# Three first attention tiles in another layout, with the first weight slice converted among their masks

## The chip, the cores and the metric

The kernel runs on one core of a Trainium2 chip. That core has five engines that run side by side and wait for each other through semaphores: PE (matrix products; PEld is its loading of weights), DVE (VectorE), ACT (ScalarE), POOL (GpSimd) and SP, which here only issues transfers (DMAs). Each engine takes its instructions in the order in which they were written. The metric is the device time of the whole kernel in microseconds (us).

## What is computed

The reference has three parts, one after the other:

```python
for t in range(S):                      # attention with decay, per batch and head
    cur = u * kt (x) vt
    y[:, :, t] = rt @ (state + cur)
    state = w * state + kt (x) vt
x = (silu(x @ w_gate) * (x @ w_val)) @ w_out          # 3072 x 384, d_ff 1536
...
e_idx = argmax(x @ gate)                              # 8 experts, one for each token
out[mask] = gate_w * eom * (relu(x[mask] @ w1[e]) @ w2[e])
```

Batch 4, 8 heads of 48, 768 positions: 3072 tokens, 24 tiles of 128. What matters here is the term with `u`, called the bonus: a token's own key and value count with the factor `u`, so a score matrix of a tile has, on its diagonal, the sum over the 48 features of r * u * k, and above it the decayed scores of the earlier tokens of the tile.

## The kernel before

Attention runs over tiles of 128 tokens. For a tile, the transposed keys and queries (features on the partitions) are scaled by powers of the decay `w` (table `WT`, built by `decay_tables` on DVE), PE makes the scores of 8 heads in two PSUM banks (`a_scores`), the diagonal of bonus sums is laid into `at` (`a_diag`: identity times the sum of a head, eight rows on ACT or one operation on POOL), DVE copies the scores over it where the mask allows (`a_mask`), and PE multiplies with v (`a_out_mm`, head pair 3 first, since its result is spread by ACT and a shift product over the three other pairs). ACT's cast and DVE's difference (`a_out_ev`) split the result into a high and a low half for the first FFN. Its twelve weight slices come as 64-bit words; DVE turns each into 32 bits (`conv_steps`: three steps of three integer operations), ACT and POOL split it (`conv_b`), PE turns its gate part (`gate_a`, `gate_b`).

Tiles 0 to 2 are handled before the first FFN block, in a layout of their own: the keys of odd and even heads lie in two separate halves with zeros in the other rows, so a score product uses all 128 rows, and each tile takes two scalings, of 1024 and of 512 columns (`a_scale`). The bonus sums are made from natural r and k, token by token: two POOL products (`a_bonus`) and a DVE sum. Later tiles have one scaling, and their score products use 64 rows each.

No planner sets the order: under `manual_schedule` each engine does its work in the order of the calls in the main function, and inside the blocks in the order of the lists `slots`. Transfers stand in SP's order, and a transfer there waits for its target to be free. Numbers behind names in the rows of the order are buffers: `bank_61` to `bank_68` are the PSUM banks 0 to 7. The names used below: `krT`, `kr3` scaled keys and queries; `rkv` natural r, k, v; `kp`, `Wk` the table that scales natural keys for the state, made by `key_table`; `raw` a weight slice as loaded, `cv` converted.

## Time and profile before

| | us |
|---|---|
| median of three runs | 863.32 (859.99 to 863.79) |
| profiled execution | 861.56 |
| its span | 859.8 |
| PE busy in the span | 821.9 (96%) |
| DVE / ACT / POOL busy | 459.8 / 271.2 / 267.9 |

The profile is of one execution. Times in it count from the start of its span; 1.76 us lie around the span. A busy share over the whole span is a mean over stages with different limits, so the rows below are read by stretches: the start with three attention tiles, the stretch in which DVE converts the weight slices, and the rest.

### The profile page before, as it was taken

Reading aid. Unit: us, or ns where it says so; the run is one execution under the profiler, and the core shown is the slowest. Engines: PE = TensorE matmul, PEld = TensorE weight load, DVE = VectorE, ACT = ScalarE, POOL = GpSimd, SP = SyncE. Lnnn points to the kernel's source line nnn. Section 1 sums busy time; section 2 is a strip of 40 time slices with the busy share of each in tenths; the row PEclk is TensorE's granted clock in tenths of the full one; section 3 lists DMA queues with packets and bytes.
Section 4 is the critical chain, followed back from the end, with each engine's and each line's share of the span. In section 5 each row is a group of like instructions: output and inputs, shape, how many; then the busy total and the mean of one; then the engine's idle time right before and its main releaser. Section 6 shows DMA issues by size and latency. Waiting matters only on the chain.

```text
span 859.8 us, 13873 instructions
## 1 busy us (share of the span) xinstructions
PE 821.9 (96%) x5427; PEld 792.9 (92%) x5427; DVE 459.8 (53%) x945; ACT 271.2 (32%) x590; POOL 267.9 (31%) x241
## 2 busy tenths in 40 slices
PE   2888889999999999999999999999999999999996
PEld 2677789999999999999999999999999999999996
DVE  7898753354465456456455434243565565465541
ACT  2434342221222212212212221223454454444432
POOL 6756546223425335245244112010110210121022
PEclk9879989999999999999999999999999999999999
DMA  8615413853322323333323210410394444444201
GB/s 249 247 59 209 146 67 100 249 141 123 105 94 78 129 78 107 109 102 130 116 102 130 60 47 29 161 51 1 118 368 142 167 142 127 158 133 163 85 26 36
DMA packets 29769, 104.90 MB, mean 122 GB/s; under 512 B 5175, under 2 KB 14193, under 8 KB 26624
## 3 DMA queue, kind: packets, MB, share of 16 engines
q1 hardware_dynamic: 26368, 94.37, 34.0%
q0 software_dynamic: 3328, 9.56, 2.9%
q8 instruction: 45, 0.74, 0.4%
q14 instruction: 28, 0.23, 0.1%
HBM read 85.84 MB, written 16.41 MB: 119 GB/s over the span
## 4 chain that ended last, share of the span: by engine, by line
PE 84%; DVE 8%; DMA 2%; issue 2%; ACT 1%; SPq 1%; POOL 0%; POOLq 0%; DVEq 0%; ACTq 0%
PE bank L494 31%; PE bank L513 17%; PE bank L708 12%; PE bank L725 12%; PE bank L363 3%; PE bank L390 2%; PE bank L376 2%; DVE bank L215 2%; DVE bank L214 2%; DMA spare<-in_rkv_dram 2%; DVE cv L216 2%; PE bank L673 1%; PE bank L739 1%; SPq L415 1%; DVE krT L316 1%
## 5 line engine op out<-in xcount | busy, mean ns | idle before, releaser
L494 PE MATMUL bank<-xT,W 128*128 128x384 f32 x1728 | 331.4, 342 | 1.5 <-DMA xT<-stage 1.3
L494 PEld LDWEIGHTS bank<-xT,W 128*128 128x128 f32 x1728 | 305.1, 189 | 5.8 <-DMA xT<-stage 2.2
L513 PE MATMUL bank<-W,h 128*128 128x400 f32 x864 | 176.0, 348 | 0.0
L513 PEld LDWEIGHTS bank<-W,h 128*128 128x128 f32 x864 | 155.9, 189 | 0.5 <-issue 0.2
L505 ACT CAST h<-s 128x384 fp32r<-128x384 f32 x96 | 49.2, 513 | 328.4 <-DVE s L503 328.4
L503 DVE TENSOR_TENSOR s<-s,bank 128x384 f32<-128x384 f32 x96 | 53.2, 554 | 161.4 <-PE bank L494 148.6
L725 PE MATMUL bank<-hd,wf 128*128 128x416 f32 (+1 forms) x576 | 113.9, 344 | 0.0
L725 PEld LDWEIGHTS bank<-hd,wf 128*128 128x128 f32 x576 | 104.3, 188 | 0.7 <-DVE hd L712 0.2
L747 POOL DMA_INDIRECT out_dram<-yo,ix x32 | 35.0, 1095 | 200.6 <-DVE yo L743 174.0
L343 POOL TENSOR_TENSOR at<-ident,a 128x1024 f32<-128x1024 f32 x19 | 36.1, 1897 | 149.2 <-PE bank L494 118.2
L712 DVE SCALAR_TENSOR_TENSOR hd<-bank,hd 128x416 fp32r<-128x416 f32 (+1 forms) x64 | 36.7, 573 | 77.1 <-ACT hd L711 77.1
L506 DVE TENSOR_TENSOR h<-s,h 128x384 fp32r<-128x384 f32 x84 | 51.8, 616 | 48.7 <-ACT h L505 48.7
L657 DVE TENSOR_TENSOR wf<-raw,wf 128x768 fp32r<-128x768 f32 x64 | 61.1, 955 | 7.0 <-ACT wf L656 1.2
L502 ACT ACTIVATE s<-bank 128x384 f32<-128x384 f32 x96 | 47.2, 492 | 47.4 <-PE bank L494 47.4
L575 POOL DMA_INDIRECT xs<-rows,slot x24 | 23.8, 991 | 112.8 <-DVE slot L573 51.5
L711 ACT ACTIVATE hd<-bank 128x416 fp32r<-128x416 f32 (+1 forms) x64 | 32.3, 505 | 82.3 <-PE bank L708 81.9
L708 PE MATMUL bank<-xd1h,wf 128*128 128x416 f32 x192 | 58.2, 361 | 0.0
L656 ACT CAST wf<-raw 128x768 fp32r<-128x768 f32 x64 | 52.8, 825 | 0.0
L368 DVE COPY_PREDICATED at<-mask,bank 128x512 f32<-128x512 int32 x42 | 28.5, 732 | 38.7 <-POOL at L343 35.3
L708 PE MATMUL bank<-xd0h,wf 128*128 128x416 f32 x144 | 43.8, 362 | 0.0
L708 PEld LDWEIGHTS bank<-xd1h,wf 128*128 128x128 f32 x192 | 36.0, 188 | 0.5
L324 POOL TENSOR_TENSOR rkv<-rkv,ub 128x384 f32<-128x384 f32 x21 | 21.8, 1037 | 46.3 <-DMA rkv<-in_rkv_dram 46.3
(175 smaller groups left out, 946.9 us busy)
## 6 DMA issues: line engine op xcount, KB each, us to landing
raw<-in_w_dram SPq DMA_DIRECT2D x36, 768.0 KB, 4.4
raw<-in_w_dram SPq DMA_DIRECT2D x22, 1152.0 KB, 7.1
rkv<-in_rkv_dram SPq DMA_DIRECT2D x21, 576.0 KB, 5.4
krT<-in_krT_dram SPq DMA_DIRECT2D x42, 192.0 KB, 3.4
xs<-zt SPq DMA_DIRECT2D x32, 197.0 KB, 6.0
xr<-xs SPq DMA_DIRECT2D x6, 591.0 KB, 5.7
spare<-in_w_dram SPq DMA_DIRECT2D x2, 1152.0 KB, 9.4
xT<-stage SPq DMA_DIRECT2D x42, 48.0 KB, 2.1
```

The lines of the kernel that those rows point to most:

```text
L343: pool.tensor_tensor(out=af, in0=bc(ident, 1, [P, NH, P]), in1=bc(a, 2, [P, NH, P]), op=ALU.mult)
L494: pe.matmul(ps[i], W[f][:, wl, o : o + P], x[:, xl, c, :], start=(c == 0 and n == 0), stop=(c == KC - 1 and n == 2),)
L502: act.activation(out=s, in_=g, func=AF.Silu)
L503: dve.tensor_tensor(out=s, in0=s, in1=v, op=ALU.mult)
L505: act.copy(out=h[:, 0], in_=s)
L506: (pool if blk == 0 else dve).tensor_tensor(out=h[:, 1], in0=s, in1=h[:, 0].bitcast(F32), op=ALU.subtract)
L513: pe.matmul(bank[t][:, 0 : DM + 16], h[:, hl, t * P : (t + 1) * P], W[f][:, wl, 2 * KC * P :], start=(f == 0 and n == 0), stop=(f == NF - ...
L656: act.copy(out=wf[:, 0], in_=raw[:, f])
L657: dve.tensor_tensor(out=wf[:, 1], in0=raw[:, f], in1=wf[:, 0].bitcast(F32), op=ALU.subtract)
L708: pe.matmul(ps, wf[:, wl, c * P : (c + 1) * P], xd[xl][:, c, 0:n], start=(i == 0), stop=(i == 3 * KC - 1))
L712: dve.scalar_tensor_tensor(h[:, 1, 0:n], ps, 0.0, h[:, 0, 0:n].bitcast(F32), ALU.max, ALU.subtract)
L725: pe.matmul(bank[c][:, 0:n], wf[:, wl, o : o + P], h[:, hl, 0:n], start=(f == 0 and i == 0), stop=(f == NEF - 1 and i == 2),)
```

## The change

Tiles 0 to 2 get the layout of the later tiles: odd and even heads in the two halves of the rows, one load for each half, one scaling of 1024 columns, score products of 64 rows. Natural r is not loaded for them. The bonus sums come from the scaled k and r: POOL multiplies the two (`pr3`), and PE sums over the features with four products a tile whose other operand is `uw`, u times w, into eight columns of bank 7 (`a_same`); a copy takes them out (`a_same_copy`). The natural v and k come as loads of their own behind the first weight slice. The three tiles go in step through scaling, scores, sums, diagonals, masks and outputs, and the three conversion steps of weight slice 0 stand among the masks and outputs. The table `kp` and `Wk`, and two of four memsets of the state, are made later; the memset of the third tile's buffer goes from POOL to DVE.

```diff
+    uT = cst.tile([P, 4], F32, name="uT")
+    uw = cst.tile([P, 4, 2], F32, name="uw")
...
-    kr3 = [spare[NF - 1 - i][:, 0 : 12 * P].rearrange("s (a p t) -> s a p t", a=3, p=4) for i in range(3)]
+    kr3 = [spare[NF - 1 - i][:, 0 : 8 * P].rearrange("s (a p t) -> s a p t", a=2, p=4) for i in range(3)]
+    pr3 = [spare[NF - 1 - i][:, 8 * P : 12 * P].rearrange("s (p t) -> s p t", p=4) for i in range(3)]
...
         act.activation(out=rev, in_=rev, func=AF.Silu)
+        dve.memset(uT, 0.0)
+        dve.memset(uw, 0.0)
         dve.memset(kr3[0], 0.0)
         pool.memset(kr3[1], 0.0)
...
-        sp.dma_start(out=ub, in_=u_d.rearrange("h d -> (h d)").partition_broadcast(P))
+        a_load_kr(0)
+        for j in range(2):
+            sp.dma_start(out=uT[64 * j : 64 * j + HD, :], in_=u_d.rearrange("(p j) d -> j d p", j=2)[j])
+        dve.memset(kr3[2], 0.0)
...
         pool.memset(cnt, 0.0)
-        pool.memset(kr3[2], 0.0)
         pool.memset(spare[4][:, 0 : 6 * P], 0.0)
...
+        for j in range(2):
+            q = slice(64 * j, 64 * j + 64)
+            dve.tensor_tensor(out=uw[q, :, j], in0=uT[q], in1=pw[q, 0, :, 0], op=ALU.mult)
...
     def a_load_kr(i):
         n = a_tile(i)
-        if i < 3:
-            t = kr3[i]
-            att[i] = {"k": (t[:, 0], t[:, 2]), "r": t[:, 1]}
-            sp.dma_start(out=t[0:HD, 0:2], in_=krT_d[n, 0])
-            sp.dma_start(out=t[64 : 64 + HD, 2], in_=krT_d[n, 1, :, 0])
-            sp.dma_start(out=t[64 : 64 + HD, 1], in_=krT_d[n, 1, :, 1])
-        else:
-            att.setdefault(i, {}).update({"k": krT[:, 0], "r": krT[:, 1]})
-            for j in range(2):
-                sp.dma_start(out=krT[64 * j : 64 * j + HD], in_=krT_d[n, j])
+        t = kr3[i] if i < 3 else krT
+        att.setdefault(i, {}).update({"k": t[:, 0], "r": t[:, 1]})
+        for j in range(2):
+            sp.dma_start(out=t[64 * j : 64 * j + HD], in_=krT_d[n, j])
 
     def a_load(i):
-        if i < 3:
-            rkv = spare[NF - 4 - i][:, 0 : 3 * DM].rearrange("s (a c) -> s a c", a=3)
-        else:
-            rkv = apool.tile([P, 3, DM], F32, tag="rkv", name="rkv", bufs=2)
+        rkv = apool.tile([P, 3, DM], F32, tag="rkv", name="rkv", bufs=2)
         sp.dma_start(out=rkv, in_=rkv_d[a_tile(i)])
         att.setdefault(i, {}).update({"rn": rkv[:, 0], "kn": rkv[:, 1], "vn": rkv[:, 2]})
 
-    def a_scale(i, parts=(0, 1)):
-        if i >= 3:
-            dve.tensor_tensor(out=krT, in0=krT, in1=WT, op=ALU.mult)
-        elif 0 in parts:
-            dve.tensor_tensor(out=kr3[i][:, 0:2], in0=kr3[i][:, 0:2], in1=WT, op=ALU.mult)
-        if i < 3 and 1 in parts:
-            dve.tensor_tensor(out=kr3[i][:, 2], in0=kr3[i][:, 2], in1=WkT, op=ALU.mult)
+    def a_load_part(i, n):
+        t = spare[NF - 4 - i][:, n * DM : (n + 1) * DM]
+        sp.dma_start(out=t, in_=rkv_d[a_tile(i)][:, n])
+        att[i]["rkv"[n] + "n"] = t
+
+    def a_scale(i):
+        t = kr3[i] if i < 3 else krT
+        dve.tensor_tensor(out=t, in0=t, in1=WT, op=ALU.mult)
+
+    def a_same(i):
+        pool.tensor_tensor(out=pr3[i], in0=kr3[i][:, 0], in1=kr3[i][:, 1], op=ALU.mult)
+        m = bank[7][:, i * 8 : (i + 1) * 8].rearrange("s (j p) -> s p j", j=2)
+        for p in range(4):
+            pe.matmul(m[:, p], pr3[i][:, p], uw[:, p], start=True, stop=True)
+        a = apool.tile([P, NH], F32, tag="a3", name="a3", bufs=3)
+        att[i]["a"] = a
+
+    def a_same_copy(i, on_act):
+        (act.copy if on_act else dve.tensor_copy)(out=att[i]["a"], in_=bank[7][:, i * 8 : (i + 1) * 8])
 
     def a_bonus(i):
         t = att[i]
 
     def a_diag(i, on_act):
         t = att[i]
-        a = apool.tile([P, NH], F32, tag="a", name="a", bufs=2)
         if i < 3:
+            a = t["a"]
             at = spare[NF - 4 - i][:, 3 * DM : 3 * DM + 8 * P].rearrange("s (j p t) -> s j p t", j=2, p=4)
         else:
+            a = apool.tile([P, NH], F32, tag="a", name="a", bufs=2)
             at = apool.tile([P, 2, 4, P], F32, tag="at", name="at", bufs=1)
-        dve.tensor_reduce(
-            out=a.rearrange("s (j p) -> s p j", j=2), in_=t["rn"].rearrange("s (p j d) -> s p j d", p=4, j=2),
-            op=ALU.add, axis=AX.X,
-        )
+            dve.tensor_reduce(
+                out=a.rearrange("s (j p) -> s p j", j=2), in_=t["rn"].rearrange("s (p j d) -> s p j d", p=4, j=2),
+                op=ALU.add, axis=AX.X,
+            )
         af = at.rearrange("s j p t -> s (j p) t")
         if on_act:
             for h in range(NH):
...
                 in1=Wk.rearrange("s (h d) -> s h d", h=NH), op=ALU.mult,
             )
 
-    def a_scores(i, b0=6):
+    def a_scores(i, b=(6, 7)):
+        k, r = att[i]["k"], att[i]["r"]
         for p in range(4):
             for j in range(2):
                 q = slice(64 * j, 64 * j + 64)
-                k, r = att[i]["k"], att[i]["r"]
-                k, r = (k[j][:, p], r[:, p]) if i < 3 else (k[q, p], r[q, p])
-                pe.matmul(bank[b0 + j][:, p * P : (p + 1) * P], k, r, start=True, stop=True)
-
-    def a_mask(i, b0=6):
+                pe.matmul(bank[b[j]][:, p * P : (p + 1) * P], k[q, p], r[q, p], start=True, stop=True)
+
+    def a_mask(i, b=(6, 7)):
         at = att[i]["at"]
         for j in range(2):
             dve.copy_predicated(
-                at[:, j], bc(mask, 1, [P, 4, P]), bank[b0 + j].rearrange("s (p t) -> s p t", p=4)
+                at[:, j], bc(mask, 1, [P, 4, P]), bank[b[j]].rearrange("s (p t) -> s p t", p=4)
             )
 
     def a_past(i, b):
 
     with tc.manual_schedule():
         setup_consts()
+        a_load_kr(1)
+        a_load_kr(2)
+        next_w(0)
         for i in range(3):
-            a_load_kr(i)
-            a_load(i)
-        for f in range(3):
-            next_w(f)
+            a_load_part(i, 2)
+        next_w(1)
+        for i in range(3):
+            a_load_part(i, 1)
+        sp.dma_start(out=ub, in_=u_d.rearrange("h d -> (h d)").partition_broadcast(P))
+        next_w(2)
         sp.dma_start(out=G, in_=g_d)
         decay_tables()
-        for b in range(2):
-            pool.memset(Sst[b], 0.0)
-        a_bonus(0)
-        a_scale(0)
-        a_scores(0, 0)
-        a_bonus(1)
-        a_scale(1, (0,))
+        sc = ((0, 1), (2, 3), (4, 6))
+        for i in range(3):
+            a_scale(i)
+            a_scores(i, sc[i])
+            a_same(i)
+        a_same_copy(0, True)
         a_diag(0, True)
-        a_scale(1, (1,))
-        a_scores(1, 2)
-        a_bonus(2)
-        a_scale(2)
-        a_diag(1, True)
-        a_mask(0, 0)
-        a_out_mm(0, 6, (3,))
-        a_scores(2, 4)
-        a_diag(2, False)
-        a_out_mm(0, 6, (0, 1, 2))
-        a_mask(1, 2)
-        a_mask(2, 4)
         steps = conv_steps(0)
-        a_out_ev(0, 6)
         steps[0]()
-        a_out_mm(1, 0, (3,))
+        a_same_copy(1, False)
+        a_same_copy(2, False)
+        a_diag(1, False)
+        a_diag(2, True)
+        a_mask(0, sc[0])
+        a_out_mm(0, 0, (3,))
+        steps[1]()
+        conv_b(0, (GV,))
+        a_mask(1, sc[1])
+        a_out_mm(1, 1, (3,))
+        a_out_mm(0, 0, (0, 1, 2))
+        a_mask(2, sc[2])
+        a_out_mm(2, 2, (3,))
+        a_out_mm(1, 1, (0, 1, 2))
+        a_out_ev(0, 0)
+        steps[2]()
+        a_out_mm(2, 2, (0, 1, 2))
+        a_out_ev(1, 1)
+        a_out_ev(2, 2)
+        gate_a(0)
+        conv_b(0, (OUT,))
         key_table()
-        a_out_mm(2, 1, (3,))
-        a_out_mm(1, 0, (0, 1, 2))
-        steps[1]()
-        a_out_mm(2, 1, (0, 1, 2))
-        steps[2]()
-        a_out_ev(1, 0)
         pool.memset(krT, 0.0)
         for i in range(3):
             a_keys(i)
-        for b in (2, 3):
+        for b in range(NB):
             pool.memset(Sst[b], 0.0)
-        conv_b(0, (GV,))
-        a_out_ev(2, 1)
-        gate_a(0)
-        conv_b(0, (OUT,))
         a_load(3)
         a_load_kr(3)
         next_w(3)
```

On DVE, between the last scaling and the first weight slice, before (`spare_101` to `spare_99` are the score matrices `at` of tiles 0 to 2):

```order
L334 TENSOR_REDUCE a<-spare_100 128x4x2 [waits DMAHW2_49,Pool_49]
L368 COPY_PREDICATED spare_101<-mask,bank_61 128x512 [waits PE_49,Activation_49]
L368 COPY_PREDICATED spare_101<-mask,bank_62 128x512 [waits PE_49,Activation_49]
L334 TENSOR_REDUCE a<-spare_99 128x4x2 [waits DMAHW6_49,DVE_49,Pool_49]
L368 COPY_PREDICATED spare_100<-mask,bank_63 128x512 [waits PE_49,Activation_49]
L368 COPY_PREDICATED spare_100<-mask,bank_64 128x512 [waits PE_49,Activation_49]
L368 COPY_PREDICATED spare_99<-mask,bank_65 128x512 [waits PE_49,Pool_49]
L368 COPY_PREDICATED spare_99<-mask,bank_66 128x512 [waits PE_49]
L411 TENSOR_TENSOR xT<-bank_67,xT 128x3x128 [waits Activation_49]
L214 TENSOR_SCALAR bank_66<-raw 128x384 [waits DMAHW7_49,DVE_49]
L215 SCALAR_TENSOR_TENSOR bank_66<-raw,bank_66 128x384 [waits DVE_49]
L216 SCALAR_TENSOR_TENSOR cv<-raw,bank_66 128x384 [waits DVE_49]
```

And now (`spare_103` to `spare_101` are those matrices, `a_215` and `a_230` the sums of tiles 1 and 2):

```order
L322 TENSOR_TENSOR spare_104<-spare_104,WT 128x1024 [waits DMAHW1_49,DMAHW0_49]
L224 TENSOR_SCALAR bank_66<-raw 128x384 [waits DMAHW2_49]
L225 SCALAR_TENSOR_TENSOR bank_66<-raw,bank_66 128x384 [waits DVE_49]
L226 SCALAR_TENSOR_TENSOR cv<-raw,bank_66 128x384 [waits DVE_49]
L333 COPY a_215<-bank_68 128x8 [waits Activation_49]
L333 COPY a_230<-bank_68 128x8
L381 COPY_PREDICATED spare_103<-mask,bank_61 128x512 [waits Activation_49,Pool_49]
L381 COPY_PREDICATED spare_103<-mask,bank_62 128x512 [waits Activation_49]
L224 TENSOR_SCALAR bank_66<-raw 128x384 [waits DVE_49]
L225 SCALAR_TENSOR_TENSOR bank_66<-raw,bank_66 128x384 [waits DVE_49]
L226 SCALAR_TENSOR_TENSOR cv<-raw,bank_66 128x384 [waits DVE_49]
L381 COPY_PREDICATED spare_102<-mask,bank_63 128x512 [waits Pool_49]
```

The first step of slice 0 now stands ahead of all masks, the second behind the first tile's masks; the two copies of sums wait for ACT.

On ACT, the first copy of sums and the work behind it, now (`a_200` are the sums of tile 0):

```order
L333 COPY a_200<-bank_68 128x8 [waits PE_49]
L355 ACTIVATE spare_103<-ident,a_200 128x128 [waits Activation_49,Pool_49]
L355 ACTIVATE spare_103<-ident,a_200 128x128 x7
L355 ACTIVATE spare_101<-ident,a_230 128x128 [waits DVE_49]
L355 ACTIVATE spare_101<-ident,a_230 128x128 x7
L410 COPY spare_99<-bank_61 48x128 [waits PE_49,Pool_49]
L410 COPY spare_99<-bank_61 48x128
L242 CAST W_264<-cv 128x768 [waits DVE_49]
L410 COPY spare_99<-bank_62 48x128 [waits PE_49]
```

The count that the first copy waits for on PE's semaphore is the one that the last bonus product of tile 2 sets, since all three tiles' sums lie in one bank. ACT has two diagonals and the cast of slice 0 in a row with the copies for the shift products.

On POOL, behind the last diagonal, before:

```order
L169 TENSOR_TENSOR kp<-WT,pw 128x512
L843 MEMSET krT 128x1024
L352 TENSOR_TENSOR spare_104<-spare_101,Wk 128x8x48
L352 TENSOR_TENSOR spare_103<-spare_100,Wk 128x8x48
L352 TENSOR_TENSOR spare_102<-spare_99,Wk 128x8x48
L847 MEMSET S_108 128x512
L847 MEMSET S_109 128x512
L233 TENSOR_TENSOR W_311<-cv,W_311 128x768
L233 TENSOR_TENSOR W_311<-cv,W_311 128x384
```

And now:

```order
L243 TENSOR_TENSOR W_264<-cv,W_264 128x768
L243 TENSOR_TENSOR W_264<-cv,W_264 128x384
L179 TENSOR_TENSOR kp<-WT,pw 128x512
L861 MEMSET krT 128x1024
L366 TENSOR_TENSOR spare_106<-spare_103,Wk 128x8x48
L366 TENSOR_TENSOR spare_105<-spare_102,Wk 128x8x48
L366 TENSOR_TENSOR spare_104<-spare_101,Wk 128x8x48
L865 MEMSET S_108 128x512
L865 MEMSET S_109 128x512
L865 MEMSET S_110 128x512
L865 MEMSET S_111 128x512
L337 TENSOR_TENSOR rkv<-rkv,ub 128x384
```

The split of slice 0 (`W_311`, now `W_264`) has moved from behind the table, the three key products and the memsets to in front of them.

## Rows read from the trace of the kernel before

**Rows 1.** Busy time by stage: PE, PEld, DVE, ACT, POOL, clock, DMA share, GB/s.

```profile
28.50:118.90 90.40, 76.54 (x539) 68.02 (x536) 78.29 (x146) 36.73 (x90) 57.17 (x49) 0.91 0.41 147
118.90:859.80 740.90, 732.04 (x4814) 713.94 (x4812) 360.81 (x756) 226.75 (x477) 192.78 (x165) 1.00 0.35 113
```

**Rows 2.** Waits of DVE, 28.5 to 119 us: total us, times, longest.

```profile
DVE xT L411 <- ACT xT L410: 6.5, 3, 2.7
```

**Rows 3.** Order of time, start: start, us, engine, line, operation, idle before.

```profile
3.51 2.35 DVE L151 TENSOR_SCALAR pw<-wT 128x4 f32<-128x4 f32 x1 [0.82 <-DMA wT<-in_w_dram]
...
3.79 1.38 POOL L139 MEMSET spare<- 128x1536 f32 x1
...
5.10 0.73 POOL L140 MEMSET spare<- 128x768 f32 x1
...
9.52 0.17 DVE L165 TENSOR_TENSOR pw<-pw 128x8 f32<-128x8 f32 x1
```

**Rows 4.** Order of time: scaling on DVE, products on GpSimd.

```profile
9.61 1.22 DVE L318 TENSOR_TENSOR spare<-spare,WT 128x1024 f32<-128x1024 f32 x1
...
12.37 0.99 POOL L325 TENSOR_TENSOR spare<-spare 128x384 f32<-128x384 f32 x1
...
12.51 1.93 DVE L318 TENSOR_TENSOR spare<-spare,WT 128x1024 f32<-128x1024 f32 x1 [1.08 <-DMA spare<-in_krT_dram]
...
23.99 1.05 POOL L169 TENSOR_TENSOR kp<-WT,pw 128x512 f32<-128x512 f32 x1
```

**Rows 5.** Busy time of L363 alone (PE, PEld, clock, DMA), then order of time.

```profile
12.25:14.75 2.50, 2.50 (x15) 2.44 (x13) 1.00 1.02 224
15.75:17.25 1.50, 1.50 (x14) 1.44 (x13) 1.00 0.99 387
...
53.60:55.40 1.80, 1.80 (x16) 1.73 (x16) 0.55 0.00 0
...
37.90 0.74 PE L249 MATMUL bank<-G,gt 128*128 128x16 f32 x6
...
49.13 1.46 PE L249 MATMUL bank<-G,gt 128*128 128x16 f32 x6
...
87.89 1.16 PE L363 MATMUL bank<-krT 64*128 64x128 f32 x14 [0.36 <-ACT gt L243]
```

**Rows 6.** Order of time: diagonals, masks, outputs of the first tiles.

```profile
14.94 2.45 ACT L341 ACTIVATE spare<-ident,a 128x128 f32<-128x128 f32 x8 [12.53 <-DVE a L334]
...
25.26 1.34 DVE L368 COPY_PREDICATED spare<-mask,bank 128x512 f32<-128x512 int32 x2 [1.62 <-PE bank L363]
...
30.14 0.49 PE L387 MATMUL bank<-spare 128*128 128x128 f32 x2
...
30.91 0.49 PE L387 MATMUL bank<-spare 128*128 128x128 f32 x2
...
33.35 0.48 ACT L410 CAST xT<-bank 128x384 fp32r<-128x384 f32 x1 [0.44 <-PE bank L390]
33.75 1.01 DVE L411 TENSOR_TENSOR xT<-bank,xT 128x384 fp32r<-128x384 f32 x2
...
34.68 0.55 DVE L214 TENSOR_SCALAR bank<-raw 128x384 int32<-128x384 int32 x1
```

**Rows 7.** Order of time: the first FFN products and after.

```profile
34.81 3.24 PE L494 MATMUL bank<-xT,W 128*128 128x384 f32 x17 [0.21 <-DVE xT L411]
...
38.98 0.83 ACT L232 CAST W<-cv 128x768 fp32r<-128x768 f32 x1
...
43.11 3.25 PE L494 MATMUL bank<-xT,W 128*128 128x384 f32 x9
...
46.24 0.56 DVE L503 TENSOR_TENSOR s<-s,bank 128x384 f32<-128x384 f32 x1
```

**Rows 8.** Busy time by stretch, columns as in Rows 1.

```profile
5.00:16.00 11.00, 4.54 (x22) 4.20 (x23) 9.14 (x30) 1.06 (x4) 5.82 (x10) 1.00 1.00 244
16.00:26.00 10.00, 6.32 (x40) 5.09 (x39) 7.56 (x10) 4.24 (x15) 8.07 (x7) 0.83 1.00 412
```

## The prediction

> **What bounds the kernel now.** I read the busy time by stages first, then who waits for whom, and then the order of time in the first 50 us. From 118.9 us on the matrix engine is busy 732.04 of 740.90 us [rows 1]: nothing that moves instructions about before that makes this stage shorter, it can only begin sooner or later. From 28.5 to 118.9 us VectorE (DVE) is the busy one, 78.29 of 90.40 us, PE is idle for 13.86 us, and the longest wait of DVE is one of 6.5 us in three pieces, for ScalarE's cast of an attention output [rows 1, 2]. That stage is the chain of integer conversions of twelve weight slices: where DVE waits in it, it waits for work that DVE itself let go a moment earlier. So its length is fixed, and what the change is worth is read at one point: when DVE begins slice 1, at 34.68 us [rows 6], and whether PE can feed it after that. Before that point lies the attention of tiles 0 to 2 and, at its end, slice 0.
>
> **The change, part by part.**
>
> *Tables.* DVE's first table operation starts at 3.51 us when its data lands and ends at 5.86; its shape is 128x4, and GpSimd's run of memsets ends at 5.83 [rows 3]. I read the 2.35 us as DVE kept out by GpSimd. GpSimd's run gets shorter: the first memset has 1024 columns instead of 1536 (1536 take 1.38 us, so 0.46 less), and the second of 1536 (1.38) goes to DVE, where it fits before 3.51. So the operation ends 1.84 us earlier, and the tables at 7.85 instead of 9.69. Two tiny products for the bonus follow (about 0.2 us each, an estimate from the 0.17 us of the last table row): 8.3. Bounds: 8.3, or 10.1 if the 2.35 us was something else. The Trainium skill ("SBUF — State Buffer", section "SBUF: two separate sides") has VectorE and GpSimd share one port pair as an exclusive lock for a whole instruction. Read strictly, DVE would have got in between the two memsets, at 5.17, and would now get in near 3.4, a gain of 0.6 us more; the trace shows it kept out by the whole run, so I go by the trace.
>
> *Scaling.* Three products of 1024 columns replace three of 1024 and three of 512. Alone one takes 1.22 us; beside a GpSimd product it takes 1.93, which is the GpSimd product's remainder and then its own time [rows 4]. GpSimd's new product of scaled k and r has 512 columns: 1.05 us by the row of that size [rows 4]. The two engines take turns: DVE 8.3 to 9.5 and 9.5 to 10.75, GpSimd to 11.8, DVE to 13.0. The key loads are 1.15 MB instead of 2.9 MB with the natural r, k and v in front; at the 244 GB/s of 5 to 16 us [rows 8] they need 4.7 us from about 3.5, so they no longer bind, and slice 0, 1.2 MB at 412 GB/s [rows 8] behind them, lands by about 12. The six small loads behind it are wanted ten and more us later.
>
> *Scores and bonus on PE.* A tile is 16 rows of scores and now 8 more rows for four bonus products. Scores with half the rows of the array cost 1.80 us per 16 at a granted clock of 0.55 (the lower of the two levels, 1.2 of 2.4 GHz, for nearly all of it), the slow pace, and 1.16 per 14, so 1.33, at the fast one [rows 5]. The bonus products have no row; the nearest are the gate products, six rows of 128x16 in 0.74 us at the fast and 1.46 at the slow pace [rows 5]: 1.0 and 1.95 for eight. From below the bound is nothing. In the trace of before the first tile runs at 15 rows in 2.5 us and the second at 14 in 1.5, with a granted clock of 1.00 in both records [rows 5]; I let the first tile run at the slow pace and the others at the fast. Tile 0: 9.6 to 11.5, wait for the product at 11.8, bonus to 13.8. Tile 1 to 16.2, tile 2 to 18.6. Bounds 15.2 (bonus free) and 21.5 (all slow).
>
> *Diagonals and masks.* In the built order the first copy of bonus sums, on ScalarE, waits for the last bonus product of tile 2, not for its own; the other two copies, on DVE, wait for ScalarE. So slice 0's first step, moved in front of them, is free (it ends at 15), but DVE then stands still. Copy 0.2 us, eight diagonal rows 2.45 [rows 6]: 21.3. Before, ScalarE began its first diagonal at 14.94. Masks are 0.67 each [rows 6]; a conversion step is three operations, 1.8 with the gaps. Half of mask 0 is done when the diagonal ends: 22.0, step 1 to 23.8, mask 1 to 25.2.
>
> *Outputs.* PE's order is now one pair of tile 1, three pairs of tile 0, one of tile 2, three of tile 1, three of tile 2. One pair with its shift product costs 0.77 us, from one such start to the next [rows 6]; a lone pair 0.4. So 0.4 + 2.3 + 0.4 + 2.3 + 2.3 after 25.2: 32.9. PE has been nearly idle since 18.6, and before, too, the stretch from 16 to 26, with a gap in PE, shows a granted clock of 0.83 in the mean [rows 8]; I add 1.2 for that (bounds 0 and 3.9, which is 0.56 of 6.9, the ratio of the two paces). 34.1. Casting the last tile, 0.48, and DVE's difference, half of 1.01 [rows 6], with 0.1 at each handover: slice 1 starts at 35.4. DVE's last step of slice 0 is hidden in there. Against 34.68: **+0.7 us**. The nine operations of 0.55 us and their gaps that leave the end of the start come back as DVE's waiting.
>
> *Behind it.* The key table is moved behind slice 0's last split on GpSimd, and its transposes stand ahead of the first FFN products on PE. From 34.1: turning the gate about 0.5, two ScalarE copies of 0.48, GpSimd's split 1.0 and table 1.05 [rows 4], transposes 0.7 with handovers: the first FFN product starts near 38.7, against 34.81 [rows 7]. Of its 18 products 17 took 3.24 us; at the slow pace, at which nine took 3.25, all take up to 6.5 [rows 7]. Then the gate products (0.74 to 1.46), ScalarE's copies and casts of slice 1 (0.83 [rows 7], and half as much for the rest), the gate copy and the sigmoid, 1.0: the gate value is there between 46 and 48.4. DVE's product with it stands 11.56 us behind the start of slice 1 (46.24 before [rows 7]), so at 47.0. Cost 0 to 1.4; I take **+0.4**. GpSimd, late by the table, the three key products, four state memsets and tile 3's bonus, delivers the low half of slice 1 some 6 us later than before, near 48; PE wants it for the last three of the nine that ended at 46.36 before. DVE asks for their result behind a scaling and a whole slice of conversion, so not before 54. Tile 3's key loads now wait for a GpSimd memset near 39, and SP issues slices 3 to 5 behind them; slice 3 is in by about 46 and is wanted after the product at 47. Free, unless the lag doubles.
>
> **Sum.** +0.7 + 0.4 = +1.1 us on the profiled execution's 861.56. The median shown is 863.32; I put the base between the two, 862.4, and forecast **863.5 us**. Half a per cent, 4.3 us, is about what a measurement of this kernel can tell from no change.
>
> **Rivals.**
>
> *Faster: the bonus products cost almost nothing and PE has the fast pace.* Two columns are far fewer than 16, which speaks for it; that six gate rows cost as much as 0.74 us, with a weight load each, speaks against. Then tile 2 is through at 15.2, 3.4 us sooner, the outputs lose their 1.2 and the lag its 0.4: 862.4 + 1.1 - 5.0 = 858.5 us. With only half of it 861.
>
> *Slower: PE keeps the slow pace through the start.* Place: scores and bonus to 21.5 (+2.9), outputs (+2.7 beyond my 1.2), first FFN products late at the sigmoid (+1.0): 863.5 + 6.6 = 870.1 us. It decides from about half of that, 4.3 - 1.1 = 3.2 us. For it: PE's work in the start is now cut by three waits, and in the trace of before the granted clock is 0.55 in a busy stretch of PE at 53.6 and the first tile crawls [rows 5]. Against it: the second tile of before was fast after a shorter wait. The Trainium skill ("TensorE: Matmul & The Clock Gate", section "What's actually happening") says that the throttled clock is the default and activity releases it. The slow first tile agrees, though its granted clock is recorded as 1.00.
>
> *The tables are not earlier.* If GpSimd was not what kept DVE, everything is 1.8 us later: 865.3. For it: the table operation outlasted a pause between two memsets.
>
> **Chances.** My forecast (860.5 to 865) 0.61, faster rival 0.18, slower rival 0.15, late tables 0.06. Over half a per cent faster needs most of the faster rival: 0.10, and 0.03 for a step that I have left out; over half a per cent slower takes two thirds of the slower rival, 0.10, and 0.03 from the tables and the lag together. Faster 0.13, same 0.74, slower 0.13. The range runs from all of the faster rival to the middle of the slower one, 858.5 to 868; the forecast's own is 860.5 to 865.
>
> **What would show it.** In the profile after: the first table operation short and the tables done by 8.5; DVE idle for some 4 us between slice 0's first step and the first mask, with ScalarE's copy of the sums as releaser near 19; DVE idle again before slice 1's start at about 35; the first FFN product near 38 to 39 behind the key table; and after 55 us everything within 2 us of its old place. I am wrong if slice 1 starts before 32 or after 38, or if DVE waits for PE between 45 and 60 us by more than a microsecond.

## The result and the profile after

The changed kernel takes 871.05 us (median of 4 runs, 870.71 to 871.39), the kernel before 862.69 (four runs now, 859.99 to 863.79): ratio 1.0102, 95% interval 1.0077 to 1.0126. It is slower by 8.4 us; 863.5 was forecast, and the range ended at 868. The profiled execution took 870.71 us, its span is 869.0 against 859.8.

From the end of the last conversion on, at 128.15 us, after has 740.85 us of PE's stage, where the kernel before has 740.90 behind 118.90 [rows 1]. The window of after (columns as in Rows 1):

```profile
128.15:869.00 740.85, 731.67 (x4814) 713.93 (x4812) 362.66 (x756) 226.52 (x477) 191.32 (x165) 1.00 0.35 113
```

So the loss lies ahead of it. The order of time of after on DVE, PE and ACT, up to the first diagonal (start, us, engine, line, operation, idle before and its releaser):

```profile
3.51 0.60 DVE L158 TENSOR_SCALAR pw<-wT 128x4 f32<-128x4 f32 x1 [0.23 <-DMA wT<-in_w_dram]
...
7.77 0.17 DVE L172 TENSOR_TENSOR pw<-pw 128x8 f32<-128x8 f32 x1
...
9.52 2.08 PE L376 MATMUL bank<-spare 64*128 64x128 f32 x16 [9.52 <-DVE spare L322]
11.78 1.87 PE L328 MATMUL bank<-uw,spare 128*128 128x2 f32 x8 [0.19 <-POOL spare L325]
13.58 2.08 PE L376 MATMUL bank<-spare 64*128 64x128 f32 x16
15.59 1.86 PE L328 MATMUL bank<-uw,spare 128*128 128x2 f32 x8
17.38 2.08 PE L376 MATMUL bank<-spare 64*128 64x128 f32 x16
19.39 1.86 PE L328 MATMUL bank<-uw,spare 128*128 128x2 f32 x8
21.30 0.17 ACT L333 COPY a<-bank 128x8 f32<-128x8 f32 x1 [18.89 <-PE bank L328]
21.49 0.24 DVE L333 COPY a<-bank 128x8 f32<-128x8 f32 x2 [6.35 <-ACT a L333]
```

The tables are done at 7.94, as forecast: DVE's first operation takes 0.60 us where it took 2.35 [rows 3]. But all three tiles' scores take 2.08 us and all bonus products 1.86, the slow pace, though PE had hardly a pause from 9.5 to 21.25. PE is through with the sums at 21.25, where 18.6 was forecast; ACT's first copy starts at 21.30, and DVE, which waits for it, stands still for 6.35 us.

The outputs of after, and what hangs on them:

```profile
28.30 0.80 PE L400 MATMUL bank<-spare 128*128 128x128 f32 x2
...
29.62 0.80 PE L400 MATMUL bank<-spare 128*128 128x128 f32 x2
...
40.66 0.90 PE L251 MATMUL bank<-ident,cv 128*128 128x128 f32 x3
40.78 0.48 ACT L423 CAST xT<-bank 128x384 fp32r<-128x384 f32 x1 [3.50 <-PE bank L403]
41.29 0.56 DVE L424 TENSOR_TENSOR xT<-bank,xT 128x384 fp32r<-128x384 f32 x1 [3.42 <-ACT xT L423]
```

From one L400 to the next are 1.33 us, where before has 0.77 [rows 6]; the nine pairs run from 28.30 to 40.66, 12.36 us. Slice 1 starts behind DVE's 41.29, at 41.77, against 34.68 [rows 6]: +7.1 us, past the 38 us that the prediction named as a sign of being wrong. From 9 to 42 us DVE waits longest for the cast of an attention output:

```profile
DVE xT L424 <- ACT xT L423: 9.7, 3, 5.0
DVE a L333 <- ACT a L333: 6.4, 1, 6.4
```

The rest comes behind. In the order of time of after, the first FFN products stand behind the key table, and at 67 us a group of down products (the second half of the FFN) is slow once more; the row below the others is the same group in the kernel before:

```profile
44.62 1.12 PE L181 MATMUL bank<-ident,kp 128*128 128x128 f32 x4 [3.06 <-POOL kp L179]
45.39 5.57 PE L507 MATMUL bank<-xT,W 128*128 128x384 f32 x18
...
65.52 0.55 PE L251 MATMUL bank<-ident,cv 128*128 128x128 f32 x3 [2.56 <-DVE at L381]
66.63 0.90 PE L259 MATMUL bank<-G,gt 128*128 128x16 f32 x6 [0.57 <-ACT gt L253]
67.37 3.35 PE L526 MATMUL bank<-W,h 128*128 128x400 f32 x9
```

```profile
59.60 1.88 PE L513 MATMUL bank<-W,h 128*128 128x400 f32 x9
```

DVE's first product with the gate value comes at 53.93, 7.7 us later than 46.24 [rows 7]; the third at 72.45, 9.3 later than before's 63.17. So: 7.1 to slice 1, 0.6 behind it, 1.6 by the third, and then both kernels run in step up to the last of the 96, here of before and, below it, of after, 9.15 us apart:

```profile
607.04 0.56 DVE L503 TENSOR_TENSOR s<-s,bank 128x384 f32<-128x384 f32 x1 [2.94 <-PE bank L494]
```

```profile
616.19 0.55 DVE L516 TENSOR_TENSOR s<-s,bank 128x384 f32<-128x384 f32 x1 [2.94 <-PE bank L507]
```

### The profile page after: what moved, and what is told of

The parts are those of the page before. It is cut to its first block, busy times and chain, and to the rows that moved or that the text cites. A ratio compares the mean times of both kernels' runs of the same rounds, so it can differ in the third digit from the quotient of the medians.

```text
span 869.0 us, 13916 instructions
## 1 busy us (share of the span) xinstructions
PE 828.9 (95%) x5451; PEld 797.9 (92%) x5451; DVE 456.1 (52%) x946; ACT 271.1 (31%) x591; POOL 262.4 (30%) x237
## 4 chain that ended last, share of the span: by engine, by line
PE 83%; DVE 6%; issue 2%; ACT 2%; DMA 1%; SPq 1%; POOL 1%; POOLq 0%; DVEq 0%; ACTq 0%
PE bank L507 31%; PE bank L526 17%; PE bank L721 12%; PE bank L738 12%; PE bank L376 2%; PE bank L403 2%; PE bank L389 2%; DVE bank L225 1%; DVE bank L224 1%; PE bank L686 1%; PE bank L752 1%; DVE cv L226 1%; SPq L428 1%; DVE s L516 1%; PE bank L440 1%
## 5 line engine op out<-in xcount | busy, mean ns | idle before, releaser
L507 PE MATMUL bank<-xT,W 128*128 128x384 f32 x1728 | 330.3, 341 | 1.6 <-DMA xT<-stage 1.6
L507 PEld LDWEIGHTS bank<-xT,W 128*128 128x128 f32 x1728 | 304.9, 189 | 5.5 <-DMA xT<-stage 2.5
L381 DVE COPY_PREDICATED at<-mask,bank 128x512 f32<-128x512 int32 x42 | 28.5, 734 | 38.6 <-POOL at L357 35.3
L243 POOL TENSOR_TENSOR W<-cv,W 128x1152 fp32r<-128x1152 f32 (+2 forms) x14 | 32.2, 2304 | 20.3 <-ACT W L242 20.3
```

What stands on the lines that cost most here:

```text
L507: pe.matmul(ps[i], W[f][:, wl, o : o + P], x[:, xl, c, :], start=(c == 0 and n == 0), stop=(c == KC - 1 and n == 2),)
```

## The experiments

Two theories. *Pace*: PE keeps the lower of its two clock levels through the start, and that is the loss. *Order*: the new chain of waits (one copy for three tiles' sums, the outputs' order, the late key table) is the loss, and the pace is hidden. In the table, the copy is ACT's first one of bonus sums (of natural sums there is none), the pair the time between two L400 (L377, L387), the last column the shift of the last of the 96 gate products against the profile of before. The e-kernels' ratios are to runs of before on the same chip. The first three columns and the shift are of one profiled execution each. Runs of before alone spread from 859.33 to 865.32 us, so a shift of 2 us by itself tells nothing. e5 and e10 fall into two groups of times, and their profiles are of the upper ones.

| kernel | copy, us | pair, us | slice 1, us | median, us | ratio (95%) | shift, us |
|---|---|---|---|---|---|---|
| before | | 0.77 | 34.68 | 862.69 | | 0 |
| after | 21.3 | 1.33 | 41.77 | 871.05 | 1.0102 (1.0077 to 1.0126) | +9.15 |
| e1_warm | 17.2 | 1.33 | 37.63 | 868.04 | 1.0058 (1.0039 to 1.0077) | +5.9 |
| e2_copy | 13.7 | 1.33 | 42.91 | 875.99 | 1.0155 (1.0139 to 1.0170) | +10.3 |
| e3_layout | | 0.77 | 31.54 | 865.94 | 1.0041 (1.0026 to 1.0057) | -0.8 |
| e4_before_warm | | 0.77 | 35.7 | 862.64 | 0.9999 (0.9982 to 1.0015) | +2.0 |
| e5_warm_both | 24.6 | 1.33, then 0.77 | 43.59 | 871.72 | 1.0101 (1.0072 to 1.0129) | +13.2 |
| e6_key | 21.3 | 1.33 | 41.8 | 870.07 | 1.0084 (1.0065 to 1.0102) | +9.9 |
| e7_scores_first | 17.3 | 1.33 | 37.74 | 867.71 | 1.0064 (1.0048 to 1.0081) | +5.7 |
| e8_warm_out | 26.1 | 0.77 | 43.87 | 872.67 | 1.0122 (1.0102 to 1.0142) | +10.2 |
| e9_first_warm | 17.5 | 0.77 | 33.87 | 863.96 | 1.0010 (0.9997 to 1.0023) | +2.0 |
| e10_scores2_late | 18.6 | 1.33 | 39.03 | 861.26 | 1.0003 (0.9978 to 1.0027) | +7.6 |
| e10_again | 16.6 | 1.33 | 37.07 | 867.06 | one run | +5.3 |
| e11_late_warm | 18.5 | 0.77 | 33.62 | 861.66 | 0.9998 (0.9984 to 1.0012) | 0.0 |
| e12_best | 16.3 | 0.77 | 31.36 | 857.69 | 0.9950 (0.9933 to 0.9968) | -4.86 |

**e1_warm.**

```diff
+    def warm(n, b):
+        for _ in range(n):
+            pe.matmul(bank[b][:, 0:P], ident, ident, start=True, stop=True)
...
         decay_tables()
+        warm(24, 0)
```

> The changed kernel with 24 extra identity-by-identity products of 128x128 on PE, into bank 0, in PE's idle time ahead of the first scores; their values are not used. Pace theory (the row-half scores and the two-column bonus products leave PE on the lower of its clock's two levels, and all of its work in the start is longer for that): the 16 scores of a tile take about 1.1 us instead of 2.08, ACT's first copy of bonus sums starts near 18 us instead of 21.3, slice 1 starts at 35 to 38 us instead of 41.8, and the time falls to 862 to 867. Order theory (the wait of the first copy for the last bonus product of tile 2, and the new order of the outputs and of the key table, make the loss; the pace of PE is hidden beside DVE and ACT): scores and bonus shorten, the start does not by more than 1.5 us, time 869.5 to 871.

PE in e1, order of time:

```profile
10.22 1.16 PE L376 MATMUL bank<-spare 64*128 64x128 f32 x16
11.78 1.05 PE L328 MATMUL bank<-uw,spare 128*128 128x2 f32 x8 [0.40 <-POOL spare L325]
...
24.17 0.80 PE L400 MATMUL bank<-spare 128*128 128x128 f32 x2
```

Nothing but 24 products without use was added, and slice 1 comes 4.1 us sooner, by as much as the copy does: the pace of scores and bonus is on the path. But PE then waits, 2.46 us for the first mask, and the outputs are slow again.

**e2_copy.**

```diff
             a_same(i)
-        a_same_copy(0, True)
+            a_same_copy(i, i == 0)
...
-        a_same_copy(1, False)
-        a_same_copy(2, False)
```

> The changed kernel with the copy of each tile's bonus sums issued right behind that tile's own bonus products, so that the first copy no longer waits for the products of tile 2. Pace theory: the first copy moves from 21.3 to about 14 us and ACT's first diagonals are done near 20, but PE's outputs keep 1.33 us for a pair's step; what is won is at most the 3 to 4 us by which masks and first outputs come earlier, and slice 1 starts at 38 to 40 us, time 867 to 870. Order theory: slice 1 starts at 35 to 37 us, time 863 to 866.

Both missed slice 1 and the time: the copy comes at 13.7, 7.6 us sooner, and slice 1 1.1 later. The edit took one wait away and put in two others, since DVE's copies now stand ahead of tile 2's scaling and of slice 0's first step. Their waits, of 7.0 and 4.0 us, are for PE's sums; tile 2's scores start at 18.93 instead of 17.38, and all outputs have 1.33 us a pair:

```profile
17.55 0.17 DVE L333 COPY a<-bank 128x8 f32<-128x8 f32 x1 [6.96 <-PE bank L328]
```

So e2 does not show what the wait for tile 2's sums is worth; e12, which keeps it, is faster than the kernel before all the same. Some 3 us of e2's time have nothing to do with the start: behind the last gate product DVE stops for 5.49 us and PE waits 2.78 us for it, as in e3 below.

**e3_layout.**

```diff
-        if i < 3:
-            t = kr3[i]
...
+        t = kr3[i] if i < 3 else krT
+        for j in range(2):
+            sp.dma_start(out=t[64 * j : 64 * j + HD], in_=krT_d[n, j])
```

(and one scaling a tile; scores from row halves)

> The kernel before with one part of the change alone: tiles 0 to 2 in the row-half layout with one scaling each and row-half score products; the bonus from natural r, the order and the loads stay. Pace theory: the second and third tile's scores take 2.1 us (before 1.5 or less), the outputs' pairs keep about 1.3 us from start to start instead of 0.77, the first products of the feed-forward stage take 5.5 us for 18 instead of 3.66, slice 1 starts 2 to 5 us later than 34.7, time 865 to 869. Order theory: the layout saves DVE two scalings and costs nothing else, slice 1 at 33 to 35 us, time 861 to 863.

PE and DVE in e3, order of time:

```profile
19.32 2.08 PE L353 MATMUL bank<-spare 64*128 64x128 f32 x16
21.33 0.80 PE L377 MATMUL bank<-spare 128*128 128x128 f32 x2
22.06 0.67 PE L380 MATMUL bank<-spare 128*48 128x128 f32 x4
22.66 0.58 PE L377 MATMUL bank<-spare 128*128 128x128 f32 x2
23.17 0.42 PE L380 MATMUL bank<-spare 128*48 128x128 f32 x4
...
636.68 0.59 DVE L702 SCALAR_TENSOR_TENSOR hd<-bank,hd 128x416 fp32r<-128x416 f32 x1 [5.68 <-issue]
```

The pace theory was wrong here: row-half scores are slow in all tiles, but the third tile's, among the outputs, are followed by the fast pace within 4 us, and slice 1 starts 3.1 us earlier than in the kernel before. The layout is a gain at the start (0.9 us of it are the tables, behind smaller memsets). The time is longer all the same: the last gate product is only 0.8 us early, and then DVE stops for 5.68 us at 631, in which the profile shows nothing that it waited for; PE waits 2.97 us for it. Of the fifteen profiles only e2's and e3's have this stop, at the same operation. Its cause is open.

**e4_before_warm.** The same `warm(24, 0)` in the kernel before.

> The kernel before with the same 24 identity products on PE ahead of its first scores. Pace theory: the first tile's scores take 1.2 us instead of 2.5, what hangs on PE in the start comes up to 1.5 us earlier, time 861 to 863. Order theory: the same, 862 to 863.5.

No difference in time, and slice 1 is 1.0 us later in the profile. The first tile's scores were not made fast throughout: PE waited 0.64 and 0.91 us for DVE's two scalings, the pace fell in the middle of the tile, and 16 rows took 2.76 us.

**e5_warm_both, e8_warm_out.** e8 has the three lines below alone, e5 also 24 ahead of the first scores; the products go to bank 7.

```diff
+        warm(12)
         a_same_copy(0, True)
...
         a_out_mm(0, 0, (3,))
+        warm(2)
...
         a_out_mm(1, 1, (3,))
+        warm(6)
```

> The changed kernel with identity products (values unused) on PE ahead of the first scores, as in e1_warm, and 20 more in the gaps that PE has behind the last bonus products and between the first outputs (12, 2 and 6). Pace theory in the form that e1_warm left (scores and bonus made fast gave 4.5 us of 7.7; the outputs were still at 1.33 us a pair): the outputs run at 0.77 us a pair, 18 pairs' steps give back 6 to 7 us, slice 1 starts near 31 to 33 us, 2 to 4 us before the kernel before; the time is 860 to 864. Order theory: the outputs are fast and slice 1 still starts at 36 us or later, since masks, copies or conversion hold it; time 866 to 868.

> The changed kernel with the 20 identity products behind the last bonus products and between the first outputs alone; none ahead of the scores. Pace theory: scores and bonus stay at 2.08 and 1.87 us, the copy at 21.3, but the outputs run at 0.77 us a pair; slice 1 starts at 35 to 37 us, time 864 to 867. Order theory: the outputs are shorter and the start is not, or by less than 1.5 us; time 869 to 871. If the dummies do not lift PE before the outputs, they only delay the first ones: 871 to 874.

The first copy and the outputs of e8, order of time:

```profile
26.08 0.17 ACT L333 COPY a<-bank 128x8 f32<-128x8 f32 x1 [23.67 <-PE bank L818]
...
35.69 0.39 PE L400 MATMUL bank<-spare 128*128 128x128 f32 x2
...
36.36 0.49 PE L400 MATMUL bank<-spare 128*128 128x128 f32 x2
```

The pace came, the time did not, and that was the experiment's fault: in bank 7 with the sums, the 12 products became what ACT's copy waits for (its releaser is now L818, the added line), 26.1 instead of 21.3. From the copy to slice 1 e8 takes 17.8 us, after 20.5, although eight added products, 4.0 us in all, stand among the outputs. e5 missed as well: its six runs fall into three of 868.6 to 869.0 us and three of 874.4 to 875.0, and in its profile the first tile's scores take 1.16 us, the second's 1.85 and the third's 2.08. So the 24 products that kept PE fast up to 17 us in e1 did not do so here.

**e6_key.** `key_table()` ahead of `gate_a(0)` and `conv_b(0, (OUT,))`.

> The changed kernel with the key table issued ahead of the gate's transposes and of the output columns' split of slice 0, so that PE no longer waits 3.06 us for GpSimd's kp. Order theory: the first product of slice 0 in the feed-forward stage starts 2 to 3 us earlier and the time falls by as much, to 868 to 869. Pace theory: slice 1's start stays at 41.8 us and DVE, which bounds the stage, gains 0 to 0.6 us by the earlier product; time 870 to 871.

PE's 3.06 us for kp are gone and L507 starts at 42.92 instead of 45.39; slice 1 and, within the measurement, the time stay. The pause was moved: PE now comes to slice 1's products before GpSimd has split that slice, waits, and is slow behind the wait, while the down products, at 67.96, are fast (1.88 us):

```profile
55.01 1.33 PE L507 MATMUL bank<-xT,W 128*128 128x384 f32 x3 [2.81 <-POOL W L243]
```

The third gate product is 0.9 us earlier than after's, the fifth no longer. So the key table by itself gives nothing that these runs can tell.

**e7_scores_first.**

```diff
             a_scores(i, sc[i])
+        for i in range(3):
             a_same(i)
```

> The changed kernel with the three tiles' scores first and the three tiles' bonus products behind them, not in turn; nothing else differs. If the two-column bonus products between the scores are what keeps PE slow, the third tile's 16 scores take about 1.2 us instead of 2.08 and the bonus 1.05 us a tile instead of 1.87; ACT's first copy starts at 17.5 to 19.5 us, and slice 1 1.5 to 3.5 us earlier than 41.8; time 867 to 869.5. If the row-half scores do not lift the pace either, all stay at 2.08 and 1.87 and the time is 870.5 to 871.5.

PE in e7, order of time:

```profile
9.53 4.51 PE L376 MATMUL bank<-spare 64*128 64x128 f32 x48 [9.53 <-DVE spare L322]
13.97 3.25 PE L328 MATMUL bank<-uw,spare 128*128 128x2 f32 x24
```

The same 72 rows in another order take 7.7 us instead of 11.7. Scores in one run lifted the pace by themselves, here and in e9; with the two-column bonus products in turn they did not in any of four profiles (after, e2, e6, e8). Slice 1 comes 4.0 us sooner.

**e9_first_warm.** e7 with `warm(6)` behind the last copy, `warm(2)` and `warm(6)` between the outputs as in e8.

> The order of e7_scores_first (scores of three tiles, then their bonus products) with 6, 2 and 6 identity products behind the last copy of bonus sums and between the first outputs, where PE would be idle; they no longer stand in front of a copy, as they did in e5_warm_both and e8_warm_out. Pace theory: the first copy starts near 17.2 us as in e7, the outputs run at 0.77 us a pair from about 23 us instead of 1.33, are done near 31, and slice 1 starts at 31 to 33 us, 9 to 10 us before the changed kernel's 41.8 and 2 to 3 before the kernel before; the time is 859 to 864. Order theory: the outputs are fast, and slice 1 starts at 36 us or later all the same; time 866 to 868.

The added products no longer delay a copy, the pair has 0.77 us, slice 1 starts at 33.87, 7.9 us before after's and 0.8 before before's. The loss is gone within the measurement: the interval allows from 0.3 us less to 2.0 us more than the kernel before. What the start won is lost again behind it: the second gate product is 0.5 us earlier than before's, the third 2.1 later, behind a wait of PE of 2.71 us for a mask and slow products:

```profile
60.02 3.35 PE L526 MATMUL bank<-W,h 128*128 128x400 f32 x9
```

**e10_scores2_late, e10_again.**

```diff
+            if i < 2:
                 a_scores(i, sc[i])
+        for i in range(3):
             a_same(i)
...
         a_out_mm(0, 0, (3,))
+        a_scores(2, sc[2])
```

> The changed kernel with the scores of tile 2 issued behind the first output of tile 0, as the kernel before has them, and the bonus products of all three tiles behind the scores of tiles 0 and 1; no product is added. Pace theory: 16 score products between the first outputs lift PE as they do in e3_layout, the outputs behind them run at 0.77 us a pair; scores of tiles 0 and 1 and the bonus stay slow, the first copy starts near 19 us, slice 1 at 33 to 36 us, time 862 to 866. Order theory: slice 1 at 38 us or later, time 868 to 871.

> e10_scores2_late once more, for a profile of one of its runs near 860 us, to be laid beside that of the run of 869.3 us: the same program. Pace theory: up to the 16 scores of tile 2 both agree within 0.5 us; the outputs behind them take 0.77 us a pair instead of 1.33, slice 1 starts 6 to 8 us earlier than 39.0 us, and nothing behind it differs by more than 2 us. If the two times have another cause, the starts agree and the difference of some 8 us lies elsewhere.

One program, two times: eight runs of 860.2 to 863.5 us, four of 868.1 to 869.3; e10_again, at 867.06, is nearer to the upper ones. Both profiles have slow outputs, e10_again with the pace risen ahead of the bonus products. PE in e10 and, below it, in e10_again, order of time:

```profile
9.52 3.79 PE L376 MATMUL bank<-spare 64*128 64x128 f32 x32 [9.52 <-DVE spare L322]
13.24 5.28 PE L328 MATMUL bank<-uw,spare 128*128 128x2 f32 x24
```

```profile
9.52 3.42 PE L376 MATMUL bank<-spare 64*128 64x128 f32 x32 [9.52 <-DVE spare L322]
12.87 2.17 PE L328 MATMUL bank<-uw,spare 128*128 128x2 f32 x16
15.22 1.33 PE L328 MATMUL bank<-uw,spare 128*128 128x2 f32 x8 [0.17 <-POOL spare L325]
```

That alone moves slice 1 from 39.03 to 37.07. A run near 860 was not profiled, so its outputs were not seen; the expectation for them is not tested.

**e11_late_warm.** e10 with six products in PE's pause ahead of the first output.

```diff
         a_same_copy(2, False)
+        warm(6)
```

> e10_scores2_late with 6 identity products on PE behind the last copy of bonus sums, where PE stood idle for 2.5 us ahead of the first output. e10 had two times, eight runs of 860.2 to 863.5 us and four of 868.0 to 869.3, and the profiled one, of the slow four, kept 1.33 us a pair through its outputs. Pace theory: with the idle time filled the outputs run at 0.77 us a pair in every run, the four slow ones go, slice 1 starts at 32 to 34 us, and all runs lie at 859 to 863 us. If something else than PE's pace makes the two times, both stay.

The outputs of e11, order of time on PE:

```profile
22.42 1.16 PE L376 MATMUL bank<-spare 64*128 64x128 f32 x16
...
25.33 0.49 PE L400 MATMUL bank<-spare 128*128 128x128 f32 x2
...
26.10 0.49 PE L400 MATMUL bank<-spare 128*128 128x128 f32 x2
...
32.52 0.55 PE L251 MATMUL bank<-ident,cv 128*128 128x128 f32 x3
```

Twelve runs, all from 859.95 to 862.97 us; the upper group is gone. Scores and bonus are as slow as in e10's first profile, the copy is at the same place, the nine pairs take 7.19 us instead of 12.37, and slice 1 starts 5.4 us sooner. Against the kernel before there is no gain, as in e9: the second gate product comes 1.7 us earlier than before's, the third, behind down products of 3.35 us, 1.1 later.

**e12_best.** e11 with `warm(24)` ahead of the first scores and the key table of e6.

> e11_late_warm with 24 identity products ahead of the first scores as well, and with the key table issued ahead of the gate's transposes and of the output columns' split. Pace theory: scores of tiles 0 and 1 at about 1.2 us and bonus at 1.05 us a tile, the first copy near 15.5 us instead of 18.6, slice 1 at 30 to 33 us, 2 to 4.5 us before the kernel before; time 857 to 861 us, which would be under both kernels. Order theory: no more than 1 us under e11.

PE in e12, order of time:

```profile
10.09 2.06 PE L376 MATMUL bank<-spare 64*128 64x128 f32 x32
12.08 1.05 PE L328 MATMUL bank<-uw,spare 128*128 128x2 f32 x8
...
30.26 0.66 PE L181 MATMUL bank<-ident,kp 128*128 128x128 f32 x4
...
31.79 3.39 PE L507 MATMUL bank<-xT,W 128*128 128x384 f32 x18
...
55.86 1.89 PE L526 MATMUL bank<-W,h 128*128 128x400 f32 x9
```

Scores, bonus, outputs and the first FFN products are fast, and so are the down products that cost after 1.5 us at 67; the slow stretch lies ahead of them now, behind a wait of PE of 3.28 us for GpSimd's split of slice 1. It beats both kernels: 0.5% under the kernel before.

## Why the prediction was wrong

- *What bounds the kernel*: right. Slice 1's start carried 7.1 us of 9.15 over, and PE's stage kept its length to 0.05 us.
- *Tables, scaling*: right. Tables at 7.94 (7.85 forecast), `uw` at 8.2 (8.3), first scores at 9.52 (9.6), the first bonus product at 11.78 (11.8). The table operation now ends at 4.11, GpSimd's memset beside it at 4.08. The pause that spoke for the rival of late tables was none: in the kernel before, the second memset starts at 5.10, the first ends at 5.17 [rows 3].
- *Scores and bonus on PE*: here it failed. The prices were near (1.80 and 1.95 forecast for a slow tile, 2.08 and 1.86 measured; 1.33 and 1.0 for a fast one, 1.16 and 1.05 in e1; the 1.16 that I scaled up from 14 rows is what 16 rows take). "I let the first tile run at the slow pace and the others at the fast" was wrong: 11.7 us instead of 9.0. I had carried the pace of before's tiles over to tiles with other products between them; e7 shows that the same rows lift it in one order and not in the other.
- *Diagonals and masks*: right. From the end of the sums to the first of the nine pairs 7.0 us were forecast and measured; 6.8 in e12.
- *Outputs*: the step was right, its size not. "I add 1.2 for that" had to be 5.2: nine pairs in 12.36 us, 8.5 forecast, 7.19 at the fast pace in e11. The upper bound of that term, 3.9, was 1.3 too low as well.
- *Sum*: 2.65 for scores and bonus and 3.9 for the outputs, less 0.2 that the last step behind them was shorter, make the 6.4 by which slice 1 came later than the 35.4 forecast. Against e12, 5.0 for the copy and 5.2 for the outputs make 10.2 of the 10.4 us between the two starts of slice 1. e12 does all the added work and products without use besides. So the added work was not the loss; the order that it was put in was, through the pace.
- *Behind it*: 0.4 forecast, 0.6 up to the first gate product, as argued. That down products 20 us later would be slow again, 1.5 us, I did not have. In e6 and e12, which move the key table, they are fast, and other products are slow in their place.
- *The slower rival* had the place, the mechanism and nearly the time, 870.1. I gave it 0.15, because before's second tile was fast "after a shorter wait". That row could not tell what the new product between two tiles would do. Nor could the granted clock: it reads 1.00 in after's slow outputs. The trace's own record of the clock begins, in every profile here, with the first rise (at 50.2 us in after, 14.3 in before, 7.1 in e1), and a stretch ahead of it reads 1.00 with nothing recorded; behind it the clock and the durations agree wherever this document uses both. L400 takes 0.80 us for two rows under that empty 1.00 in after, and under a recorded 0.50 in e1. The Trainium skill ("TensorE: Matmul & The Clock Gate", section "Seeing it yourself") warns that recorded clock events were seen to be unreliable; no run here shows a wrong event, only the missing start. The windows of after and, below it, of e1 (columns as in Rows 1):

```profile
28.00:41.00 13.00, 13.00 (x62) 7.47 (x61) 3.57 (x7) 2.21 (x7) 1.50 (x1) 1.00 0.01 2
```

```profile
28.00:41.00 13.00, 9.94 (x49) 5.70 (x45) 6.36 (x12) 2.85 (x7) 2.56 (x3) 0.50 0.00 1
```

What stays open: what e10's fast runs and e5's look like, what stops DVE behind the last gate product in e2 and e3, and how much of e12's last 4 us is the key table and how much the first 24 products.

## What to carry to other kernels

Read PE's pace from the duration of one product in each stretch, not from its busy share, and trust a granted clock of 1.00 only behind its first recorded fall. Ask of every group of small products whether the work behind it will still be fast. Put products like the scores in one run; where PE must pause ahead of work that others wait for, a few products without use, in a bank that nobody is waiting to read, can be worth more than the pause. Ask, too, where a pause goes when it is moved: e6 and e12 moved one, and with it the slow products behind it. Price an order by the pace that it leaves behind: here single products cost about what their rows said, and against e12 two terms of five microseconds came from where the products stood.

## What was not expected of the hardware

- Twelve two-column bonus products (24 rows) in turn with 48 rows of row-half scores kept PE at the low pace for 11.7 us with hardly a pause (after; the same in e6 and e8); the 48 rows of scores in one run raised it before they ended, in 4.5 us (e7, e9). Of 32 rows in one run, with bonus products behind, one profile had the rise within 3.4 us (e10_again) and two had none (e10, e11).
- PE stayed slow through 12.36 us of outputs without a pause (after), and was fast through the same outputs once it had come to them fast (e8, e9, e11).
- One program came out 8 us apart from run to run (e10). The Trainium skill (same page, section "What's actually happening") says that the number of slow products of a kernel varies by run; e10's two profiles agree, with 32 rows of scores in 3.79 and in 3.42 us.
